# Attention plus MLP on one core: the position-bias hidden layer is made per distance instead of per key column

## The chip, the cores and the metric

The program runs on one core of a Trainium2 chip. The metric is the device time of one launch in microseconds (us); the kernel before takes 705.3 us (median of three runs, 705.29 to 706.06). A core has TensorE (PE, the matrix engine; PEld are its weight loads), VectorE (DVE), ScalarE (ACT), GpSimd (POOL), and SyncE (SP), which here only issues transfers. Sixteen DMA engines move the data.

## The reference

Attention over 4 batches, 8 heads, 576 positions and 64 channels, with a learned position bias, and then a two-layer block on the result. What matters here is the bias:

```python
rel = (pos[:, None] - pos[None, :]).astype(np.float32)
psi_rel = np.log1p(np.abs(rel))
psi_i = np.log1p(np.maximum(pos[:, None].astype(np.float32), 1.0))
x = (psi_rel / psi_i)[..., None]
h = np.maximum(x @ w1 + b1, 0.0)      # 32 hidden units
bias = h @ w2                         # 8 heads
scores = scores + bias.transpose(2, 0, 1)[None, :, :, :]
```

So `bias[i, j]` depends on the row `i` and on the distance `|i - j|` alone. The softmax, the product with v and the block `h * clip(h + 3, 0, 6) / 6 @ w_out` follow.

## The kernel before, in words

The bias is the same for all batches. It is made once, written to a table in DRAM (`bias_d`, five tiles of up to 128 rows), and loaded from there tile by tile when the softmax needs it.

It is made in 36 groups of 16 rows. Dividing by `psi_i` is left to the end: the kernel takes `relu(w1 * log1p(distance) + b1 * psi_i)` and scales by `1 / psi_i` when it evicts. `T` holds `w1 * log1p(|column - 572 - a|)`, 1148 columns wide, 32 hidden units by four rows (`a`) on 128 partitions, so a slice of 576 columns that starts at `572 - i0` is the row `i0 + a` over all keys. Each group has four steps:

- `z_group` (L827): four instructions of 128 x 576, each of four rows, dealt to DVE (L837) and ACT (L841); for groups 0 to 15 they take turns, later DVE takes two of three. 85 are on DVE and 59 on ACT.
- `bias_mm` (L845, L854): TensorE multiplies by `w2`. Each of the four results `z` goes to 32 of the 128 output partitions, in two halves of 288 columns, in f32: eight products, which the chip runs as 16 weight loads and 16 matmul instructions.
- `bias_out` (L860, L870): ACT evicts with scale and bias into `bo`; one instruction of 576 columns, or two of 288 once the kernel is in its steady stage (11 groups).
- `bias_store` (L873, L876): one transfer of 288 KB from `bo` to the table, issued on ACT's queue.

Groups 0 to 15 are made in the first 53 us, beside the preparation of `w_in` (L245 to L269, L122, L139) and the first tiles of attention. The other 20 run between 166 and 300 us, between the products of the block (L772, L795). `load_bias` (L466, L486, L483) loads the table on SP's queue.

The program is written as steps on one list, and a planner orders each engine's instructions by priority and by a simulated timeline. From tile 45 on TensorE and SP keep the order of the list (`keep_order`, L1083). How often a bias step is taken is set by the rates in `CFG`. Before any of this, `T` is loaded in two transfers (L1009, L1016) and scaled by `w1` in two DVE instructions (L1024).

Of the kernel before, what the change touches and what calls it, by code (L numbers as in the profile page):

```python
# [10 lines left out]
F32 = mybir.dt.float32  # L11
# [4 lines left out]
ALU = mybir.AluOpType  # L16
AX = mybir.AxisListType

S = 576
D = 64  # L20
H = 8
PAIRS = H // 2
HALF = S // 2
LT = 1148
NG = S // 16
CQ = 2.0 ** -25
VC = 5 * 128
# [6 lines left out]
def attention_moe_kernel(  # L34
# [15 lines left out]
    nc = tc.nc  # L50
# [15 lines left out]
    hl_p = ctx.enter_context(tc.tile_pool(name="hl", bufs=5))  # L66
    sm_p = ctx.enter_context(tc.tile_pool(name="sm", bufs=6))
    dr_p = ctx.enter_context(tc.tile_pool(name="dr", bufs=1, space=bass.MemoryType.DRAM))
# [11 lines left out]
    def s_bank(name):  # L80
        return pools["ps_s"].tile([128, 2, 512], F32, tag="s", name=name)
# [6 lines left out]
    def w_bank(name):  # L88

        if name == "o_ps":  # L90
            out_open[:] = [True, 0]
        elif out_open[0] and steady[0]:
            while out_open[0] and out_open[1] == 3:
                next(queue[0])
            out_open[1] += 1
        return pools["ps_w"].tile([128, 512], F32, tag="w", name=name)
# [3 lines left out]
    r_sb = const.tile([128, 2, 2 * PAIRS * 4], F32, name="r_sb")  # L100
    wi = big.tile([128, 2, KC, DFF], F16, name="wi")
    wo = big.tile([128, 2, KF, DM], F16, name="wo")
    bias_d = [dr_p.tile([H, min(128, S - i), S], F32, name=f"bias{i}") for i in range(0, S, 128)]

    ones_sb = const.tile([1, 128], F32, name="ones_sb")
    b1_sb = const.tile([128, 1], F32, name="b1_sb")
    w2_sb = const.tile([128, 32], F32, name="w2_sb")
# [3 lines left out]
    def halves(t):  # L111
        return t.rearrange("p (a b) -> p a b", a=2)
# [110 lines left out]
    def dq(c):  # L223
        return nc.scalar if c in cfg["act"] else nc.sync
# [241 lines left out]
    def load_bias(b, p, i):  # L466
        out = b_p.tile([128, 2 * S], F32, tag="bt", name="bt")
        src = [out[:, s * S:(s + 1) * S] for s in range(2)]
        if (p, i) in KEEP:
            if b:  # L470
                return out, kept[p, i]
            tag = KEEP[p, i]
            if tag == "z":
                t = z_e[:, p // 2]
            else:
                t = (const if tag[0] == "k" else pools["e"]).tile(
                    [128, 2 * S], F32, tag=tag, name=f"k{p}{i}"
                )
            src = [t[:, s * S:(s + 1) * S] for s in range(2)]
            kept[p, i] = src  # L480
        table = bias_d[i][2 * p:2 * p + 2]
        if i == 4:
            d = dq("b").dma_start(out=out[:, 0:S], in_=table.rearrange("h i j -> (h i) j"))  # L483
        else:
            whole = t if (p, i) in KEEP else out
            d = dq("b").dma_start(  # L486
                out=whole.rearrange("i (h j) -> i h j", h=2), in_=table.rearrange("h i j -> i h j")
            )
        bias_loads.append(d.ins)
        return out, src  # L490
# [321 lines left out]
    def zeng(g, k):  # L812
        pat = cfg["zeng"] if g >= cfg["gz2"] else cfg["z1"] if g >= cfg["gz"] else cfg["z0"]
        return pat[(4 * g + k) % len(pat)]

    def pattern(g):
        return tuple(zeng(g, k) != "A" for k in range(4))
# [6 lines left out]
    bias_t = {}  # L824
    emitted = [0, 0, 0, 0]

    def z_group(g):  # L827
        zs = []
        for k in range(4):
            i0 = 16 * g + 4 * k  # L830
            col = slice(i0 // 4, i0 // 4 + 1)
            src = T[:, 572 - i0:572 - i0 + S]
            if k % 2 == 0:
                z2 = (z_a if phase == 0 and g % 2 else z_e)[:, k // 2]
            z = z2[:, (k % 2) * S:(k % 2 + 1) * S]
            if zeng(g, k) == "D":
                nc.vector.tensor_scalar(  # L837
                    out=z, in0=src, scalar1=nbp[:, col], scalar2=None, op0=ALU.max
                )
            else:  # L840
                nc.scalar.activation(out=z, in_=src, func=AF.Relu, bias=bp[:, col])  # L841
            zs.append(z)
        bias_z[g] = zs

    def bias_mm(g):  # L845
        if steady[0]:
            pss = [w_bank("b_ps") for _ in range(2)]
        else:
            ps = s_bank("b_ps")
            pss = [ps[:, 0], ps[:, 1]]  # L850
        zs = bias_z.pop(g)
        for a in range(2):
            for k, z in enumerate(zs):
                nc.tensor.matmul(  # L854
                    out=pss[a][32 * k:32 * k + 32, 0:HALF], lhsT=w2_sb,
                    rhs=z[:, a * HALF:(a + 1) * HALF],
                )
        bias_ps[g] = pss if steady[0] else ps

    def bias_out(g):  # L860
        ps = bias_ps.pop(g)
        t = hl_p.tile([128, S], F32, tag="hl", name="bo")
        c = pats.index(pattern(g))
        cv, sc = cv_sb[:, c:c + 1], isc[:, g:g + 1]
        if isinstance(ps, list):
            ev = [(t[:, a * HALF:(a + 1) * HALF], ps[a][:, 0:HALF]) for a in range(2)]
        else:
            ev = [(halves(t), ps[:, :, 0:HALF])]
        for dst, src in ev:
            nc.scalar.activation(out=dst, in_=src, func=AF.Identity, scale=sc, bias=cv)  # L870
        bias_t[g] = t

    def bias_store():  # L873
        g = emitted[3]
        r0 = (16 * g) % 128
        dq("o").dma_start(  # L876
            out=bias_d[g // 8][:, r0:r0 + 16].rearrange("h i j -> i h j"), in_=bias_t.pop(g)
        )
        emitted[3] += 1

    def bias_step():
# [13 lines left out]
    def bias_next():  # L895
        z, m, o, d = emitted
        z_group(z)
        bias_mm(m)
        emitted[0] += 1
        emitted[1] += 1  # L900
        if o < m:
            bias_out(o)
            emitted[2] += 1
            bias_store()
# [16 lines left out]
    def front(n):  # L921
# [25 lines left out]
        while len(bt_t) - freed[0] < 4 and len(bt_t) < len(keys):  # L947
            k, b, p, i = keys[len(bt_t)]
            if k - n > (cfg["la"] if n > 3 else 2):
                break  # L950
            bias_until(128 * i + 128 if i < 2 else S)
            bt_t[b, p, i] = load_bias(b, p, i)
# [48 lines left out]
    T = pools["e"].tile([128, 2 * S], F32, tag="T", name="T")  # L1001
# [4 lines left out]
    isc = pools["e"].tile([128, NG], F32, name="isc")  # L1006
    w1_sb = pools["e"].tile([128, 1], F32, name="w1_sb")
    c36 = const.tile([128, 2], F32, name="c36")
    nc.sync.dma_start(out=T[:, 512:LT], in_=ltab[:, 512:LT])  # L1009
    nc.sync.dma_start(out=w1_sb, in_=w1c)  # L1010
    nc.sync.dma_start(out=b1_sb, in_=b1c)
    nc.sync.dma_start(out=bp, in_=psi)
    nc.sync.dma_start(out=w2_sb, in_=w2b)
    nc.sync.dma_start(out=isc, in_=ipsi)
    nc.sync.dma_start(out=eye_sb, in_=eye)
    nc.sync.dma_start(out=T[:, 0:512], in_=ltab[:, 0:512])  # L1016
    nc.vector.memset(cv_sb, 0.0)
    nc.vector.memset(ones_sb, 1.0)
    nc.vector.memset(c36[:, 0:1], 3.0 * CQ)
    nc.vector.memset(c36[:, 1:2], 6.0 * CQ)  # L1020
    for r in range(2):
        nc.gpsimd.memset(tq[r].bitcast(F32), 0.0)
    for cs in (slice(512, LT), slice(0, 512)):
        nc.vector.tensor_scalar(  # L1024
            out=T[:, cs], in0=T[:, cs], scalar1=w1_sb, scalar2=None, op0=ALU.mult
        )
    nc.vector.tensor_scalar(out=bp, in0=bp, scalar1=b1_sb, scalar2=None, op0=ALU.mult)
    nc.vector.tensor_scalar(out=nbp, in0=bp, scalar1=-1.0, scalar2=None, op0=ALU.mult)
    nc.vector.tensor_scalar(out=w2_sb, in0=w2_sb, scalar1=8.0, scalar2=None, op0=ALU.mult)
# [9 lines left out]
    for c, pat in enumerate(pats):  # L1039
        for k in range(4):  # L1040
            if pat[k]:
                rows = slice(32 * k, 32 * k + 32)
# [102 lines left out]
    for n in range(-1, NT + 7):  # L1145
# [17 lines left out]
        if done is not None and done != (0, 0):  # L1163
            b, u = done
# [20 lines left out]
def _layout(q, k, v, w1, b1, w2, moe_w_in, moe_w_out):  # L1185
    import numpy as _np

    Bn = q.shape[0]
    qt, kt = (x.transpose(0, 1, 3, 2).reshape(Bn, PAIRS, 128, S) for x in (q, k))
    qk = _np.concatenate([qt[..., :256], kt, qt[..., 256:]], axis=3)  # L1190
    rows = _np.arange(128)[:, None] + 128 * _np.arange(5)[None, :]
    rows[64:, 4] -= 64
    vr = v[:, :, rows.reshape(-1), :].reshape(Bn, PAIRS, 2, 128, 5, D)
    vp = vr.transpose(0, 1, 3, 4, 2, 5).reshape(Bn, PAIRS, 128, VC)
    w1c = _np.tile(w1.reshape(32, 1), (4, 1))
    b1c = _np.tile(b1.reshape(32, 1), (4, 1))
    w2b = _np.zeros((128, 32), dtype=w2.dtype)
    for a in range(4):
        w2b[32 * a:32 * a + 32, 8 * a:8 * a + 8] = w2
    a = _np.repeat(_np.arange(4), 32)  # L1200
    col = _np.arange(LT)
    ltab = _np.log1p(_np.abs(col[None, :] - 572 - a[:, None]).astype(_np.float32))
    pos = _np.arange(S).astype(_np.float32)
    psi = _np.log1p(_np.maximum(pos, _np.float32(1.0)))
    inv = (1.0 / psi.astype(_np.float64)).astype(_np.float32)
    row = _np.arange(128)
    ipsi = inv[16 * _np.arange(NG)[None, :] + (row // 32 * 4 + row % 32 // 8)[:, None]]
    psi = psi[4 * _np.arange(S // 4)[None, :] + a[:, None]]
    d = {
        "qk": qk, "vp": vp, "w1c": w1c, "b1c": b1c, "w2b": w2b,  # L1210
        "ltab": ltab.astype(_np.float32), "psi": psi, "ipsi": ipsi,
        "eye": _np.eye(128, dtype=_np.float32),
        "w_in": moe_w_in.view(_np.int64), "w_out": moe_w_out.view(_np.int64),
    }
    return {n: _np.ascontiguousarray(d[n]) for n in _INS}
# [20 lines left out]
```

## Time and profile before

| | us |
|---|---|
| median of three runs | 705.3 |
| the profiled execution | 701.48 |
| its span, first to last instruction | 699.5 |
| TensorE busy | 647.4 (93%) |
| VectorE busy | 487.8 (70%) |
| ScalarE busy | 488.6 (70%) |
| GpSimd busy | 252.7 (36%) |
| mean granted TensorE clock | 0.98 of full speed |

The share of busy time is a mean over stages. Until some 80 us TensorE is not the busiest engine, and after 300 us it hardly stops. A table by stretches says more than the shares.

### The profile page before, as it was taken

To read this page: it belongs to the slowest core of one execution; us is meant where nothing else is said; L and a number is where in the kernel's file an instruction comes from. 1 tells how busy PE (TensorE), PEld (TensorE's weight loads), DVE (VectorE), ACT (ScalarE), POOL (GpSimd) and SP (SyncE) were. 2 spreads that over 40 slices of the span, in tenths; PEclk is the share of its full clock that TensorE was granted. 3 is DMA by queue.
4 is the path that set the end of the run, shared out by engine and by line. 5 is a ranking of instruction groups with operands and counts; after the bars stand their busy time and mean duration, and the time that the engine had idled before them with its cause. 6 is when DMAs were issued, how large, how long until landed. Compare 5 with 4: busy or idle time off the path is not lost. (4 is left out here: it accounts for less than half of the span.)

```text
span 699.5 us, 15122 instructions
## 1 busy us (share of the span) xinstructions
PE 647.4 (93%) x5538; PEld 469.3 (67%) x5538; DVE 487.8 (70%) x1159; ACT 488.6 (70%) x963; POOL 252.7 (36%) x334
## 2 busy tenths in 40 slices
PE   7566899988899999999898899999999999999998
PEld 2234566765486667688787788767776777777775
DVE  7889869998776797667777877777677767410310
ACT  7986777978756998677768776886678856621620
POOL 2113121756302443145444552565236512410420
PEclk9988999999999999999999999999999999999999
DMA  8899867750999959898999699879896776100000
GB/s 266 280 356 344 277 227 272 262 193 4 229 241 228 256 117 261 230 236 184 236 276 247 143 207 220 200 146 199 171 202 132 162 149 130 21 10 29 1 10 28
DMA packets 177017, 129.08 MB, mean 185 GB/s; under 512 B 137776, under 2 KB 146224, under 8 KB 175920
## 3 DMA queue, kind: packets, MB, share of 16 engines
q1 hardware_dynamic: 167152, 112.79, 64.4%
q10 hardware_dynamic: 9792, 15.34, 7.2%
q8 instruction: 43, 0.70, 0.4%
q14 instruction: 30, 0.25, 0.1%
HBM read 76.19 MB, written 15.34 MB: 131 GB/s over the span
## 5 line engine op out<-in xcount | busy, mean ns | idle before, releaser
L772 PE MATMUL h_ps<-x,wi 128*128 128x256 f16 (+1 forms) x1536 | 202.6, 290 | 8.6 <-DVE t L755 3.9
L795 PE MATMUL o_ps<-g,wo 128*128 128x256 f16 (+1 forms) x1536 | 195.5, 286 | 0.8 <-DVE g L120 0.4
L772 PEld LDWEIGHTS <-wi 128*128 128x128 f16 x1536 | 149.2, 99 | 56.2 <-issue 13.9
L795 PEld LDWEIGHTS <-wo 128*128 128x128 f16 x1536 | 147.3, 98 | 46.0 <-issue 8.3
L751 POOL TENSOR_TENSOR g<-t,g 128x256 f16<-128x256 f32 (+1 forms) x128 | 102.5, 810 | 135.9 <-ACT g L749 134.9
L565 ACT ACTIVATE bt<-bt,sm 128x576 f32<-128x576 f32 x144 | 110.7, 769 | 52.5 <-DVE sm L554 49.7
L139 DVE SCALAR_TENSOR_TENSOR hl<-bt,sm,hl 128x576 f16<-128x576 f32 x112 | 99.6, 903 | 25.6 <-ACT hl L122 13.1
L755 DVE SCALAR_TENSOR_TENSOR t<-t,t,h_ps 128x320 f32<-128x320 f32 (+1 forms) x112 | 56.2, 515 | 63.8 <-ACT t L762 61.8
L116 POOL TENSOR_SCALAR hl<-bt,sm 128x576 f16<-128x576 f32 x56 | 45.0, 805 | 105.6 <-DVE sm L577 59.6
L749 ACT ACTIVATE g<-t 128x256 f16<-128x256 f32 (+1 forms) x128 | 55.8, 440 | 35.9 <-DVE t L755 35.4
L554 DVE CUSTOM_DVE_ANT_0 bt<-s_ps,bt 128x576 f32<-128x576 f32 x88 | 64.8, 749 | 10.0 <-PE s_ps L542 5.2
L762 ACT ACTIVATE t<-h_ps,t,hr 128x320 f32<-128x320 f32 (+1 forms) x112 | 64.8, 586 | 8.4 <-PE h_ps L772 6.0
L411 POOL TENSOR_TENSOR qkl<-st,qkh 128x576 fp32r<-128x576 f32 (+2 forms) x48 | 55.9, 1187 | 26.1 <-ACT qkh L404 25.5
L805 ACT ACTIVATE ot<-o_ps,os 128x256 f32<-128x256 f32 (+1 forms) x32 | 15.9, 497 | 58.1 <-PE o_ps L795 54.8
L854 PE MATMUL b_ps<-z_e,w_sb 128*32 128x288 f32 x448 | 44.1, 430 | 9.9 <-ACT bo L870 4.2
L573 DVE TENSOR_SCALAR sm<-sm 128x1 f32<-128x1 f32 x112 | 16.7, 150 | 43.6 <-ACT bt L565 43.6
L520 PE MATMUL s_ps<-qk 128*128 128x288 f32 x128 | 40.2, 439 | 7.3 <-ACT atf L616 2.6
L122 ACT ACTIVATE hl<-bt,sm 128x576 f16<-128x576 f32 x56 | 43.0, 770 | 5.5 <-issue 1.2
L837 DVE TENSOR_SCALAR z_e<-T,nbp 128x576 f32<-128x576 f32 x69 | 37.8, 595 | 5.4 <-PE b_ps L854 5.4
L841 ACT ACTIVATE z_e<-T,bp 128x576 f32<-128x576 f32 x43 | 32.0, 767 | 7.9 <-PE b_ps L854 4.1
L542 PE MATMUL s_ps<-qkh 64*128 64x288 f32 x192 | 30.4, 346 | 6.6 <-DVE sm L554 6.3
L870 ACT ACTIVATE bo<-b_ps,cv_sb,isc 128x576 f32<-128x576 f32 (+1 forms) x47 | 33.2, 709 | 4.2 <-DMA at<-hl 2.2
(128 smaller groups left out, 881.9 us busy)
## 6 DMA issues: line engine op xcount, KB each, us to landing
bt<-bias SPq DMA_DIRECT2D x36, 576.0 KB, 5.3
bias<-bo ACTq DMA_DIRECT2D x36, 288.0 KB, 5.4
w<-in_w_in_dram SPq DMA_DIRECT2D x8, 1024.0 KB, 6.6
vs<-in_vp_dram SPq DMA_DIRECT2D x24, 320.0 KB, 4.9
st<-in_qk_dram SPq DMA_DIRECT2D x16, 448.0 KB, 4.3
wo<-in_w_out_dram SPq DMA_DIRECT2D x5, 1024.0 KB, 7.1
bt<-bias SPq DMA_DIRECT2D x16, 288.0 KB, 3.7
va<-in_vp_dram SPq DMA_DIRECT2D x12, 320.0 KB, 6.3
```

The lines of the kernel that those rows point to most:

```text
L116: nc.gpsimd.tensor_scalar(out=out, in0=full, scalar1=scale, scalar2=1.0, op0=ALU.mult, op1=ALU.mult)
L139: nc.vector.scalar_tensor_tensor(out=out, in0=full, scalar=scale, in1=high, op0=ALU.mult, op1=ALU.subtract)
L411: nc.gpsimd.tensor_sub(out=lo[:, c:c + w], in0=t[:, c:c + w], in1=hi[:, c:c + w].bitcast(F32))
L554: nc.vector.tensor_tensor_reduce(out=halves(bt), in0=ps, in1=halves(src), op0=ALU.add, op1=ALU.min, scale=-0.125, scalar=3.0e38, accum_out ...
L565: nc.scalar.activation(out=bt, in_=bt, func=AF.Exp, scale=-1.0, bias=sm[:, 0:1], accum_out=total)
L749: nc.scalar.activation(out=g[:, 0], in_=uu, func=AF.Copy)
L751: e.tensor_sub(out=g[:, 1], in0=uu, in1=g[:, 0])
L755: nc.vector.scalar_tensor_tensor(out=t_t[f], in0=t_t[f], scalar=cols(f)[2], in1=h_t.pop(f)[:, 0:n], op0=ALU.min, op1=ALU.mult,)
L762: nc.scalar.activation(out=t_t[f], in_=h_t[f][:, 0:n], func=AF.Relu, scale=cols(f)[0], bias=cols(f)[1],)
L772: nc.tensor.matmul(out=h_t[f][:, 0:n], lhsT=wi[:, a, c, f * 128:(f + 1) * 128], rhs=x[:, e, c], start=(k == 0), stop=(k == 3 * KC - 1),)
L795: nc.tensor.matmul(out=ops[:, 0:n], lhsT=wo[:, a, f, e * 128:(e + 1) * 128], rhs=g_t[f][:, r], start=(f == 0 and a == 0 and r == 0), stop= ...
L854: nc.tensor.matmul(out=pss[a][32 * k:32 * k + 32, 0:HALF], lhsT=w2_sb, rhs=z[:, a * HALF:(a + 1) * HALF],)
```

## The change

The hidden layer is now taken over distances 0 to `w - 1`, where `w` is one more than the largest distance in the group: `576 - 16g` for groups 0 to 17, `16g + 16` from 18 on. `T` shrinks to 576 columns, the same in all four rows of a partition group. The product reads `z` backwards for the keys on the left of the diagonal and forwards for those on the right, 591 columns in all, and cuts them where the direction turns and where a PSUM bank ends: two pieces for groups 4 to 31, three for the other eight. Row `r` of a group then stands shifted by `r`; the store undoes that by stepping one element more per row in a DRAM table whose rows are 608 wide.

```diff
-LT = 1148
+BW = S + 15
+BP = 608
...
-    bias_d = [dr_p.tile([H, min(128, S - i), S], F32, name=f"bias{i}") for i in range(0, S, 128)]
+    bias_d = [dr_p.tile([H, min(128, S - i), BP], F32, name=f"bias{i}") for i in range(0, S, 128)]
...
-        table = bias_d[i][2 * p:2 * p + 2]
+        table = bias_d[i][2 * p:2 * p + 2, :, 16:16 + S]
...
-            src = T[:, 572 - i0:572 - i0 + S]
+            w = max(16 * g + 15, S - 1 - 16 * g) + 1
+            src = T[:, 0:w]
...
-            z = z2[:, (k % 2) * S:(k % 2 + 1) * S]
+            z = z2[:, (k % 2) * S:(k % 2) * S + w]
...
+    def bias_cut(g):
+        left = 16 * g + 15
+        return left, min(max(left, BW - 512), 512)
...
-        for a in range(2):
+        left, first = bias_cut(g)
+        cuts = sorted({0, left, first, BW})
+        for lo, hi in zip(cuts, cuts[1:]):
+            c = 512 - first + lo if lo < first else lo - first
             for k, z in enumerate(zs):
                 nc.tensor.matmul(
-                    out=pss[a][32 * k:32 * k + 32, 0:HALF], lhsT=w2_sb,
-                    rhs=z[:, a * HALF:(a + 1) * HALF],
+                    out=pss[int(lo >= first)][32 * k:32 * k + 32, c:c + hi - lo], lhsT=w2_sb,
+                    rhs=z[:, left - lo:left - hi:-1] if lo < left else z[:, lo - left:hi - left],
                 )
...
-        t = hl_p.tile([128, S], F32, tag="hl", name="bo")
+        t = hl_p.tile([128, BW], F32, tag="hl", name="bo")
...
+        first = bias_cut(g)[1]
         if isinstance(ps, list):
-            ev = [(t[:, a * HALF:(a + 1) * HALF], ps[a][:, 0:HALF]) for a in range(2)]
+            ev = [(t[:, 0:first], ps[0][:, 512 - first:]), (t[:, first:], ps[1][:, 0:BW - first])]
         else:
-            ev = [(halves(t), ps[:, :, 0:HALF])]
+            ev = [(t, ps.rearrange("p a b -> p (a b)")[:, 512 - first:512 - first + BW])]
...
-        dq("o").dma_start(
-            out=bias_d[g // 8][:, r0:r0 + 16].rearrange("h i j -> i h j"), in_=bias_t.pop(g)
-        )
+        rows = bias_d[g // 8][:, r0:r0 + 16, 1:1 + BW].rearrange("h i j -> i h j")
+        step, *rest = rows.ap
+        dst = bass.AP(rows.tensor, rows.offset, [[step[0] + 1, step[1]], *rest])
+        dq("o").dma_start(out=dst, in_=bias_t.pop(g))
...
-    nc.sync.dma_start(out=T[:, 512:LT], in_=ltab[:, 512:LT])
+    nc.sync.dma_start(out=T[:, 0:S], in_=ltab)
...
-    nc.sync.dma_start(out=T[:, 0:512], in_=ltab[:, 0:512])
...
-    for cs in (slice(512, LT), slice(0, 512)):
-        nc.vector.tensor_scalar(
-            out=T[:, cs], in0=T[:, cs], scalar1=w1_sb, scalar2=None, op0=ALU.mult
-        )
+    nc.vector.tensor_scalar(out=T[:, 0:S], in0=T[:, 0:S], scalar1=w1_sb, scalar2=None, op0=ALU.mult)
```

## Rows read from the trace of the kernel before

**Rows 1.** The page's first part: busy time, share, instructions of each engine.

```profile
PE 647.4 (93%) x5538; PEld 469.3 (67%) x5538; DVE 487.8 (70%) x1159; ACT 488.6 (70%) x963; POOL 252.7 (36%) x334
```

**Rows 2.** Busy time by stretch (us from the start); the first line names the columns.

```profile
core 0: us, PE busy (x) PEld busy (x) DVE busy (x) ACT busy (x) POOL busy (x), PEclk, DMA share, GB/s
0.00:30.00 30.00, 21.16 (x172) 8.19 (x176) 24.50 (x58) 24.79 (x33) 7.05 (x17) 1.00 0.87 296
30.00:40.00 10.00, 3.68 (x44) 1.33 (x36) 7.25 (x11) 8.12 (x13) 1.20 (x1) 0.74 0.74 250
40.00:80.00 40.00, 30.50 (x176) 19.05 (x169) 39.72 (x88) 31.65 (x52) 8.36 (x10) 0.89 0.91 328
80.00:100.00 20.00, 20.00 (x138) 12.26 (x136) 13.81 (x39) 14.32 (x26) 4.27 (x6) 1.00 0.74 251
100.00:160.00 60.00, 54.89 (x389) 41.17 (x388) 56.26 (x122) 50.10 (x95) 28.04 (x24) 0.97 0.66 229
160.00:180.00 20.00, 17.03 (x140) 11.42 (x139) 18.18 (x41) 15.03 (x30) 9.83 (x11) 0.91 0.19 39
180.00:300.00 120.00, 112.78 (x1133) 81.00 (x1133) 87.31 (x216) 91.69 (x177) 38.22 (x48) 0.99 0.95 226
300.00:700.00 400.00, 387.34 (x3367) 294.87 (x3365) 240.79 (x588) 252.94 (x543) 155.72 (x219) 1.00 0.66 145
```

**Rows 3.** Waits of DVE from 4 to 52 us: total, times, longest.

```profile
DVE bt L554 <- DMA bt<-bias: 2.7, 1, 2.7
...
DVE vparts L178 <- DMA vf<-in_vp_dram: 1.4, 1, 1.4
```

**Rows 4.** Groups of instructions, shapes kept apart: count | busy, mean ns | idle before.

```profile
L837 DVE TENSOR_SCALAR z_e<-T,nbp 128x576 f32<-128x576 f32 x69 | 37.8, 595 | 5.4 <-PE b_ps L854 5.4
L841 ACT ACTIVATE z_e<-T,bp 128x576 f32<-128x576 f32 x43 | 32.0, 767 | 7.9 <-PE b_ps L854 4.1 <-DVE bp L1027 2.9 <-DVE w2p L162 0.8
L870 ACT ACTIVATE bo<-b_ps,cv_sb,isc 128x576 f32<-128x576 f32 x25 | 20.4, 821 | 3.3 <-DMA at<-hl 2.2 <-PE b_ps L854 1.0
...
L870 ACT ACTIVATE bo<-b_ps,cv_sb,isc 128x288 f32<-128x288 f32 x22 | 12.8, 582 | 0.9 <-ACT ot L805 0.5 <-DMA bias<-bo 0.2 <-PE b_ps L854 0.2
...
L1024 DVE TENSOR_SCALAR T<-T,w_sb 128x636 f32<-128x636 f32 x1 | 0.6, 550 | 2.3 <-DMA w_sb<-in_w1c_dram 2.3
L1024 DVE TENSOR_SCALAR T<-T,w_sb 128x512 f32<-128x512 f32 x1 | 0.5, 478 | 0.0
```

**Rows 5.** Timeline at the start, SP and DVE: start us, us, instruction.

```profile
4.01 0.43 SPq L1016 DMA_DIRECT2D T<-in_ltab_dram  x1
...
6.93 0.48 DVE L1024 TENSOR_SCALAR T<-T,w_sb 128x512 f32<-128x512 f32 x1
```

**Rows 6.** Bias products from 160 to 300 us: durations ns min/median/max, first and last start.

```profile
L854 PEld LDWEIGHTS b_ps<-z_e,w_sb x320: 106/109/178, 169.0 to 296.9; 128*32 128x32 f32 x160
L854 PE MATMUL b_ps<-z_e,w_sb x320: 406/406/689, 169.0 to 297.2; 128*32 128x288 f32 x160
```

**Rows 7.** Timeline: one group's products (start us, us; 16 instructions merged).

```profile
250.35 1.18 PE L854 MATMUL b_ps<-z_e,w_sb 128*32 128x288 f32 x16
```

**Rows 8.** Waits of PE from 160 to 300 us: total, times, longest.

```profile
PE b_ps L854 <- DVE z_e L837: 2.1, 2, 1.1
PE b_ps L854 <- ACT bo L870: 1.8, 1, 1.8
PE b_ps L854 <- ACT z_e L841: 0.8, 1, 0.8
```

**Rows 9.** The page's transfers: issuer, count, KB each, median us to landing.

```profile
bt<-bias SPq DMA_DIRECT2D x36, 576.0 KB, 5.3
bias<-bo ACTq DMA_DIRECT2D x36, 288.0 KB, 5.4
...
T<-in_ltab_dram SPq DMA_DIRECT2D x1, 318.0 KB, 2.9
T<-in_ltab_dram SPq DMA_DIRECT2D x1, 256.0 KB, 2.8
```

More of the change, by code (lines that the diff above doesn't have):

```diff
@@ L1200, in _layout @@
     a = _np.repeat(_np.arange(4), 32)
-    col = _np.arange(LT)
-    ltab = _np.log1p(_np.abs(col[None, :] - 572 - a[:, None]).astype(_np.float32))
+    ltab = _np.broadcast_to(_np.log1p(_np.arange(S).astype(_np.float32)), (128, S))
     pos = _np.arange(S).astype(_np.float32)
```

## The prediction

> **What bounds the kernel now.** I read the shares first: TensorE is busy 93% of the span, DVE and ACT 70% each [rows 1]. Such a mean hides stages, so next I read busy time by stretch [rows 2]. Three regimes show. Up to 80 us TensorE is not the bound: it is busy 21.2 of the first 30 us and 3.7 of the next ten, while the DMA share is 0.87 at 296 GB/s, and from 40 to 80 us DVE works 39.7 of 40 us. From 100 to 180 us DVE is still the fullest beside TensorE (18.2 of 20 us from 160 on). From 180 us TensorE leads (112.8 of 120 us) and after 300 us it is busy 387 of 400. The bias work lies in the first regime (groups 0 to 15, up to 53 us) and from 166 to 300 us (groups 16 to 35). So what the change takes from DVE and ACT counts early, and what it adds to TensorE counts late. Then the waits: before 52 us DVE idles 2.7 us for the first bias load and 1.4 us for v [rows 3]; from 160 to 300 us TensorE waits 2.9 us, in three pieces, for `z` from DVE or ACT and 1.8 us for an eviction [rows 8].
>
> **The change part by part.**
>
> *The table T.* One load and one DVE instruction go: the second part, 0.48 us [rows 5], and 60 columns of the first. Two widths of this instruction give DVE's price per column: (550 - 478) / 124 = 0.58 ns [rows 4], so 0.03 us more; 0.51 us in all. The transfers shrink from 318 + 256 KB to 288 KB [rows 9], about 1.0 us at the 296 GB/s of that stretch [rows 2], and SP issues its first `w_in` load 0.43 us earlier [rows 5]. The first scaling does not move: it waits for `w1` [rows 4], not for T.
>
> *The hidden layer.* Instruction count stays at 144; each shrinks from 576 to `w` columns. Saved columns: 896 on DVE and as many on ACT in groups 0 to 7 (16 instructions each), 2944 each in groups 8 to 15, then 7936 on DVE (53 instructions) and 3968 on ACT (27). ACT's price per column from its evictions is (821 - 582) / 288 = 0.83 ns [rows 4]. DVE therefore saves 0.52 + 1.71 + 4.60 us and ACT 0.74 + 2.44 + 3.29 us. The bounds of a column on DVE are 0 and 595 / 576 = 1.03 ns [rows 4], as the trace has no narrower `z`; I take 0.58, the same operation between the same memories.
>
> *What of it counts early.* The wait of 2.7 us for the first bias load [rows 3] hangs on group 7's store, so up to it only what that store gains counts: T and groups 0 to 7, about 1.0 us on DVE and 0.6 on ACT, less the longer products of groups 0 to 3 (below). I take 0.7 us. After that wait DVE is full until 80 us, and there the eight `z` of groups 12 to 15 (1728 columns) give 1.0 us. Sum 1.7 us, bounds 0 (transfers keep the pace: 328 GB/s from 40 to 80 us [rows 2]) and 0.51 + 0.52 + 1.71 = 2.7. When DVE's stretch ends earlier, TensorE, full from 80 to 100 us [rows 2], is late next, and passes the gain on.
>
> *What of it counts later.* Groups 16 to 19 lose 2896 columns on DVE, 1.7 us, in the stretch where DVE has 18.2 of 20 us; about half is on the path, 0.8 us. Behind each of TensorE's three waits for `z` [rows 8] stand about two instructions, so each wait shrinks by some 0.15 us: 0.4. Sum 1.2 us; bounds 0, and 1.7 + 2.9 = 4.6. The rest lies under TensorE's work.
>
> *The products.* A group runs as passes of four matmuls side by side. Its 16 instructions last 1.18 us [rows 7] and one matmul 0.406 [rows 6], so the four passes start (1.18 - 0.406) / 3 = 0.258 us apart: 0.9 ns per column. A group now streams 591 columns twice: +15 x 2 x 0.9 = 0.03 us. [...] Groups 16 to 35 then add 0.3 + 0.25 + 1.3 = 1.9 us, where TensorE has no cover. Bounds: 0.5 us (20 groups x 0.03, columns alone) and some 9 us, if each of the 24 short passes there took a whole 0.406.
>
> The row shows 109 ns for a weight load whatever follows it [rows 6]. [...] No row here shows a short pass.
>
> *Reading backwards.* No row has a moving operand with a negative step. Bounds: nothing, or twice the forward rate on the reversed columns, 8460 in groups 16 to 35: 8460 x 2 x 0.9 ns = 15.2 us. I take nothing, the forward rate being the only row [rows 7]; the other end is a rival.
>
> *Eviction, store, load.* Fifteen columns more are 12 ns per eviction on ACT, 0.2 us up to 53 us and under TensorE's work later. 36 stores and all loads stay in number and on their queues (ACT's and SP's); a store carries 2364 instead of 2304 bytes per row, +2.6%. The stores hold no wait that was not there: the eviction before them ends where its last product ends. I cost them at nothing as long as the landing stays near 5.4 us [rows 9].
>
> *Sum.* -1.7 - 1.2 + 1.9 = -1.0 us against the profiled 701.48, that is 700.5. The median of the runs is 3.8 us above that execution, so the forecast is 704.3. Its own range: from -2.7 - 4.6 + 0.5 to 0 + 0 + 2.2 (passes with a little more than a weight load each), 698.5 to 707.5.
>
> **The rivals.**
>
> *A. The early gain is larger.* The planner orders DVE, ACT and POOL anew with the shorter instructions and fills the holes of the first 80 us (DVE idles 5.5 us in the first 30, 2.75 from 30 to 40 [rows 2]). For: all engines wait on each other there. Against: DMA at 296 GB/s is close to the 328 of the later stretch. All of 2.7, half of the wait for the first load (1.4) and 2 of the later 4.6, less 1.9 for TensorE: -4.2 us, 701.1.
>
> *B. Reading backwards is slow.* Place: left pieces of groups 16 to 35 in TensorE's own stretch, where it idles only 7 of 120 us [rows 2]. At twice the time: 15.2 us, less the 1.0 forecast and some 2 us of idle time: +12 us, 717. It decides from a slowdown of (1.0 + 1.4) / 15.2 = 16% of the reversed columns; below that the result is no change. For: nothing measured. Against: the forward pass leaves no sign of a memory limit.
>
> *C. The gains stay covered.* The early stretch keeps the pace of its transfers, the planner's new order costs as much as it gives, and TensorE pays its 1.9 us: +2 us, 707.3.
>
> *D. Rows off the grid.* A stored row now starts at any multiple of 4 bytes, and rows are loaded 2432 bytes apart. If loads and stores took a tenth longer (5.3 and 5.4 us [rows 9]), the first load and some later ones would land 0.5 us later each: 0 net of the gains, 705.3; if a store had to wait for the one before, ACT would stand with it, up to 5 us in the first stretch: +4. The nearest row speaks against a price: T's rows were 4592 bytes apart and its 318 KB landed in 2.9 us [rows 9]. [...]
>
> *E. Short passes cost only their columns.* If weights for a short pass are in place before it is due, the products add the lower bound, 0.5 us: -1.7 - 1.2 + 0.5 = -2.4 us, 702.9. For: a weight load runs beside the matmuls of the pass before, and takes less than half of one [rows 6]. Against: a short pass leaves no time to hide the next load.
>
> *The change does nothing.* If `z` of 320 columns took as long as one of 576, only T's 0.5 us would be left against 1.9: this ends within C.
>
> **How the numbers follow.** Forecast 0.38, A 0.18, B 0.10, C 0.14, D 0.08, E 0.12. A measurement of this kernel can tell 0.2% (1.4 us) from no change. Faster by more than that (below 703.9): A, 0.11 of E and 0.12 of the forecast, whose range leans to that side, 0.41. Within: 0.25 of the forecast, 0.01 of E, 0.04 of C, 0.02 of D, 0.32. Slower: B, 0.10 of C, 0.06 of D, 0.01 of the forecast, 0.27. The range goes from 699, below A, to 710; it leaves out B, the ends of A and D, and the far end of the short passes, 0.17 together.
>
> **What would show it.** `z` of group 17 (304 columns) at about 0.36 us on DVE and 0.54 on ACT; T scaled once. Passes of 512 forward and of left pieces at 0.9 ns per column alike; short passes 0.11 us apart, groups 32 to 35 near 1.5 us to the end of the last product. The first softmax of the table some 0.7 us before 37.5 us, and TensorE's full stretch beginning 1.7 us before 80. Busy TensorE after 300 us unchanged. Wrong if reversed passes are longer than forward ones, if stores land well after 5.4 us, or if TensorE's idle time changes where no bias work is: then the order, not the work, made the difference.

## The result and the profile after

The change is slower. In five runs it took 713.15 us at the median against 705.3, a ratio of 1.0102 (95% interval 1.0058 to 1.0146), and in the first experiment 1.0110 (1.0072 to 1.0148). The profiled execution of after took 706.67 us, 6.5 below its median; so the two profiles differ by 5.2 us where the medians differ by 7.9, and ratios of many runs carry the verdicts below. One per cent is 7.0 us.

The work went down about as forecast. The page's first part of the kernel after, to be set against [rows 1]: DVE has 9.5 us less (the savings of the prediction add up to 7.3), ACT 5.8 less (6.5), TensorE 2.7 more.

```profile
PE 650.1 (92%) x5602; PEld 472.3 (67%) x5602; DVE 478.3 (68%) x1158; ACT 482.8 (69%) x963; POOL 245.2 (35%) x334
```

Busy time by stretch of the kernel after, columns as in [rows 2]; the last three lines are cut more finely than there:

```profile
0.00:30.00 30.00, 19.81 (x190) 7.17 (x192) 23.34 (x57) 23.50 (x32) 7.17 (x17) 0.90 0.86 284
30.00:40.00 10.00, 8.31 (x62) 3.60 (x56) 8.89 (x20) 9.10 (x15) 1.37 (x1) 0.80 0.79 249
40.00:80.00 40.00, 28.37 (x155) 17.63 (x156) 37.61 (x78) 29.80 (x50) 6.57 (x10) 0.79 0.92 333
160.00:180.00 20.00, 18.28 (x163) 11.74 (x165) 15.21 (x41) 13.36 (x30) 6.15 (x10) 1.00 0.20 42
180.00:300.00 120.00, 109.35 (x1087) 80.13 (x1084) 79.35 (x203) 85.47 (x168) 36.56 (x46) 0.94 0.90 217
300.00:700.00 400.00, 390.31 (x3416) 297.97 (x3417) 243.03 (x595) 255.92 (x549) 157.84 (x220) 1.00 0.68 147
...
180.00:187.60 7.60, 5.70 (x49) 2.92 (x45) 3.54 (x13) 5.39 (x12) 1.35 (x2) 1.00 1.20 271
187.60:201.20 13.60, 10.53 (x51) 7.09 (x51) 11.11 (x35) 10.26 (x18) 6.12 (x6) 0.50 0.86 220
201.20:300.00 98.80, 93.12 (x990) 70.13 (x990) 64.70 (x157) 69.82 (x140) 29.09 (x38) 1.00 0.89 212
```

TensorE's busy time from 180 to 300 us fell from 112.8 to 109.4 although it has more to do there, and within that, from 187.6 to 201.2 us, its clock was granted at 0.50 of full speed, after it had stood idle for 1.67 us up to 187.39. Where is it held up? The timeline of the kernel after, by engine (DVE, ACT, POOL, PE):

```profile
187.25 0.15 DVE L160 COPY p_w<-m_ps 128x1 f32<-128x1 f32 x1
...
190.50 1.95 DVE L141 SCALAR_TENSOR_TENSOR hl<-bt,sm,hl 128x576 f16<-128x576 f32 x1 [2.49 <-POOL hl L118]
192.37 0.15 DVE L219 RECIPROCAL rm_w<-p_w 128x1 f32<-128x1 f32 x1
...
195.00 0.22 DVE L221 TENSOR_SCALAR r_w2c<-w2p,rm_w 128x8 f32<-128x8 f32 x1
...
182.11 0.84 ACT L882 ACTIVATE bo<-b_ps,cv_sb,isc 128x591 f32<-128x591 f32 x1 [3.51 <-DMA at<-hl]
...
195.87 0.71 ACT L124 ACTIVATE g<-g,r_w2c 128x512 f16<-128x512 f16 x1
...
189.72 0.75 POOL L118 TENSOR_SCALAR hl<-bt,sm 128x576 f16<-128x576 f32 x1 [4.18 <-DMA bias<-bo]
...
187.39 0.71 PE L544 MATMUL s_ps<-qkh 64*128 64x288 f32 x2 [1.67 <-DVE sm L556]
...
190.85 2.20 PE L865 MATMUL b_ps<-z_e,w_sb 128*32 128x335 f32 x16 [1.79 <-ACT bo L882]
194.33 0.84 PE L544 MATMUL s_ps<-qkh 64*128 64x288 f32 x2 [1.28 <-DVE sm L556]
...
197.75 4.47 PE L797 MATMUL o_ps<-g,wo 128*128 128x256 f16 x24
```

The same place in the kernel before (ACT, DVE, POOL, PE):

```profile
180.99 0.83 ACT L870 ACTIVATE bo<-b_ps,cv_sb,isc 128x576 f32<-128x576 f32 x1 [2.21 <-DMA at<-hl]
...
187.93 0.16 DVE L158 COPY p_w<-m_ps 128x1 f32<-128x1 f32 x1 [1.62 <-PE m_ps L155]
...
188.55 0.23 DVE L219 TENSOR_SCALAR r_w2c<-w2p,rm_w 128x8 f32<-128x8 f32 x1
...
188.57 0.77 POOL L116 TENSOR_SCALAR hl<-bt,sm 128x576 f16<-128x576 f32 x1 [2.62 <-PE m_ps L155]
...
191.50 0.50 PE L795 MATMUL o_ps<-g,wo 128*128 128x256 f16 x3
```

`r_w2c` scales `g`, and `g` opens the second layer's products `o_ps`. From `p_w`, which it comes from, to `r_w2c` DVE took 0.62 us before and takes 7.75 now, though `p_w` is ready 0.7 us earlier. In between stand two `z`, a split tile `hl` that waits for POOL, a reduction, a softmax and a split of v, none of them a new instruction: the planner put them there. TensorE's own order has moved too: one more group of bias products and more scores (`s_ps`) now stand ahead of `o_ps`, and they wait 1.67, 1.79 and 1.28 us for a softmax, an eviction and a softmax. When `o_ps` starts at 197.75 us it waits for nothing, as its first `g` has stood since 196.6. So this trace does not say how much of the delay is the late `g` and how much TensorE's own queue; both are the planner's order. DVE's wait of 2.49 us for POOL comes through a shared buffer. The evicted bias tile `bo` and the split tiles (`hl`, `xr`) take turns in five buffers (tag `hl`); the eviction of group 17 waits 3.51 us until a transpose has read one of them, and POOL's next `hl` waits 4.18 us until that group's store has left it.

### The profile page after: what moved, and what is told of

The parts are those of the page before. It is cut to its first block, busy times and chain, and to the rows that moved or that the text cites. A ratio compares the mean times of both kernels' runs of the same rounds, so it can differ in the third digit from the quotient of the medians.

```text
span 704.7 us, 15238 instructions
## 1 busy us (share of the span) xinstructions
PE 650.1 (92%) x5602; PEld 472.3 (67%) x5602; DVE 478.3 (68%) x1158; ACT 482.8 (69%) x963; POOL 245.2 (35%) x334
## 5 line engine op out<-in xcount | busy, mean ns | idle before, releaser
L774 PE MATMUL h_ps<-x,wi 128*128 128x256 f16 (+1 forms) x1536 | 197.9, 286 | 7.1 <-DVE t L757 3.7
L774 PEld LDWEIGHTS <-wi 128*128 128x128 f16 x1536 | 146.9, 98 | 52.1 <-issue 11.7
L753 POOL TENSOR_TENSOR g<-t,g 128x256 f16<-128x256 f32 (+1 forms) x128 | 98.7, 781 | 130.6 <-ACT g L751 126.0
L865 PE MATMUL b_ps<-z_e,w_sb 128*32 128x512 f32 (+46 forms) x496 | 44.6, 441 | 13.2 <-ACT z_e L844 8.3
L882 ACT ACTIVATE bo<-b_ps,cv_sb,isc 128x591 f32<-128x591 f32 (+16 forms) x47 | 33.8, 720 | 9.6 <-PE b_ps L865 5.2
L865 PEld LDWEIGHTS b_ps<-z_e,w_sb 128*32 128x32 f32 x496 | 14.3, 117 | 35.4 <-ACT z_e L844 15.6
L840 DVE TENSOR_SCALAR z_e<-T,nbp 128x320 f32<-128x320 f32 (+17 forms) x69 | 32.8, 521 | 7.5 <-PE b_ps L865 7.5
```

Source lines behind the costliest of these rows:

```text
L753: e.tensor_sub(out=g[:, 1], in0=uu, in1=g[:, 0])
L774: nc.tensor.matmul(out=h_t[f][:, 0:n], lhsT=wi[:, a, c, f * 128:(f + 1) * 128], rhs=x[:, e, c], start=(k == 0), stop=(k == 3 * KC - 1),)
L865: nc.tensor.matmul(out=pss[int(lo >= first)][32 * k:32 * k + 32, c:c + hi - lo], lhsT=w2_sb, rhs=z[:, left - lo:left - hi:-1] if lo < left ...
```

## The experiments

All compare with runs of the kernel before on the same chip. Runs that are set beside each other often stand on different chips, so their ratios to before are compared, not their times. Intervals are 95%, and for a difference of two ratios I take the root of the sum of the squared half-widths. Theory T1: the planner's new order costs, not the work. Rival R1: the work costs (products, stores). Rival R2: the order costs, but in the first 100 us.

**Order and work exchanged.** At the end of the program each engine's instructions are chained in a given order, the one that the planner made for the other kernel:

```diff
+    impose_order(nc, tc)
...
+        for a, b in zip(picks, picks[1:]):
+            tc.add_manual_dep(
+                line[b], line[a].name,
+                mybir.DependencyInfo(mybir.DependencyClass.NoSync, mybir.DependencyReason.DATA),
+                reason="issue order",
+            )
```

The control lays before's own order on before.

> Control: the kernel before, with its own order laid on every engine in the way that the runs with an exchanged order had theirs. Every theory: 1.000 of before, within its interval. If it is off by 0.4% or more, laying an order on the engines costs time by itself, and the runs with an exchanged order must be read against this one.

Measured 0.9999 (0.9977 to 1.0020): laying an order on costs nothing that +-0.2% can show. Its profile also says how far one execution can be trusted: the same program in the same order has a span of 701.9 us instead of 699.5, and from 30 to 40 us its granted clock is 0.89 instead of 0.74. The others:

> The changed kernel as it is, a second time, so that the three others have it beside them on the same chip. Theory T1 (the planner's new order of instructions around 180 to 200 us, not the work, costs the time) and rival R1 (the work itself costs: reversed and three-piece products, stores and loads off the grid): both 1.010 of before again, 707 to 715 us. Its trace shows the first product into o_ps some 6 us later than in before (191.5) and a stretch at the lower granted clock between 185 and 205 us by T1.

> All the work of the change (T, narrower z, passes of two or three pieces, shifted stores and loads), but on every engine the instructions are issued in the order that they have in the kernel before; where the change has more products, they stand where their group's products stood. T1: no slower than before, 1 to 4 us faster (701 to 704 us beside 705), because the work went down by 10 us on DVE and 6 on ACT and up by 3 on TensorE; the first product into o_ps within 1 us of 191.5. R1: as slow as the changed kernel, 1.008 to 1.012 of before.

> All the work of the kernel before (576-column z, passes of 288), but on every engine in the order that the planner gave to the changed kernel. T1: slower than before by 5 to 12 us (710 to 717), with the same late o_ps and idle TensorE around 185 to 200 us. R1: 705, as before.

> The work of the change; the order of the changed kernel up to the first h_ps product (some 103 us), the order of the kernel before from there on. T1 (loss lies at 180 to 200 us): as fast as the change in the old order throughout, 700 to 704 us, perhaps 1 us faster as the weights are made earlier. Rival R2 (the loss lies in the first 100 us, where the first softmax comes 4.8 us later and the lower clock lasts longer): slower than the old order throughout by 4 us or more.

Measured: after again 1.0110; the change's work in the old order 1.0062 (1.0034 to 1.0089), 709.5 us; the old work in the new order 1.0149 (1.0116 to 1.0181), 715.0 us; new order up to 103 us, then the old one, 1.0056 (1.0026 to 1.0085). T1 is half right: the new order costs the old work 1.5% and the changed work 0.5% (+-0.5). R2 falls: the new first part costs nothing that shows (1.0056 beside 1.0062, +-0.4% on the difference). But the work in the old order is not the gain that T1 asked for; it is a loss of 0.6%, so T1 alone does not do. R1 alone does not either, as it asked for the whole 1%. About half of the loss comes with the order and half with the work.

**A buffer of its own for one bias tile.** Theory T2: the loss at 180 to 200 us comes through the shared buffers. By it their waits go and the products `o_ps` behind them come earlier: 704 to 706 us in the old order (709.5 with the shared buffer); in the new order `o_ps` some 3 us earlier and 706 to 709 us.

```diff
+        if g == 17:
+            t = const.tile([128, 2 * S], F32, tag="kb1", name="bo")[:, 0:BW]
+        else:
+            t = hl_p.tile([128, BW], F32, tag="hl", name="bo")
```

> As work_oldorder (work of the change, order of before), but the evicted bias tile of group 17 goes to a buffer of its own, one that nothing else uses before 260 us, in place of one of the five buffers that it shares with the split attention tiles. [...] Rival R1 (the products and stores themselves cost): 709, unchanged. Rival R3 (several small losses before 180 us, 2.4 us in that trace, with the lower clock): 707 to 708.

> The changed kernel in its own order, with the same one buffer for the bias tile of group 17. [...] T1 alone (the new order as such, whatever the buffers): no change, 712 to 713.

> The work and order of the kernel before, with the buffer of its own for group 17's bias tile. In the trace of before this store had landed at 188.4 us, 0.2 us ahead of the split tile that reuses its buffer, so T2 expects little: 703 to 705 us, 0.998 to 1.002. If it gains 2 us or more, the buffer is worth as much without the change, and the change is to be set against this kernel.

> The changed kernel with group 17's own buffer, in its own order up to the first h_ps product (some 103 us) and in the order of before from there. The order costs 4 us more with that buffer (707.9 against 703.9). If they are lost after 103 us (T1 with T2): 702 to 704.5 us. If before (R2): 707 to 708.5.

> The changed kernel with group 17's own buffer, where the planner makes its order anew with that buffer in view; nothing laid on the engines. If its order is free of the waits on shared buffers: 702 to 706 us. If the planner again puts the scaling of g late behind other work (T1): 707 to 712.

Measured: old order 1.0009 (0.9986 to 1.0032), new order 1.0063 (1.0035 to 1.0091), before itself 0.9955 (0.9927 to 0.9983), new order to 103 us 1.0014 (0.9984 to 1.0044), planned anew 1.0050 (1.0025 to 1.0076). The timeline of the old order with the change's work, first with the shared buffer (work_oldorder; ACT, POOL, PE):

```profile
183.32 0.84 ACT L1092 ACTIVATE bo<-b_ps,cv_sb,isc 128x591 f32<-128x591 f32 x1 [1.78 <-DMA at<-hl]
...
192.13 0.74 POOL L328 TENSOR_SCALAR hl<-bt,sm 128x576 f16<-128x576 f32 x1 [4.92 <-DMA bias<-bo]
...
191.61 0.49 PE L1007 MATMUL o_ps<-g,wo 128*128 128x256 f16 x3 [0.77 <-ACT g L334]
195.97 4.43 PE L1007 MATMUL o_ps<-g,wo 128*128 128x256 f16 x20 [3.87 <-DVE g L332]
```

and with the tile's own (oldorder_own_bo):

```profile
180.21 0.84 ACT L1095 ACTIVATE bo<-b_ps,cv_sb,isc 128x591 f32<-128x591 f32 x1
...
184.59 0.74 POOL L328 TENSOR_SCALAR hl<-bt,sm 128x576 f16<-128x576 f32 x1
...
192.26 7.94 PE L1007 MATMUL o_ps<-g,wo 128*128 128x256 f16 x56 [2.65 <-ACT g L334]
```

With the shared buffer `o_ps` begins at 191.61 us, as T1 had it, and then stands 3.87 us for the next `g`; with the tile's own it begins at 192.26 and runs on. The waits for `at<-hl` and `bias<-bo` are gone, as T2 said, and the three pairs with the change's work gain 0.42 to 0.53% (+-0.4 to 0.5 on each), some 3.3 us. But before gains as much (0.45%, +-0.28), where I expected nothing: there too the eviction stood 2.2 us for the buffer. So sharing is a cost of either kernel, not the change's own; T2 does not explain the difference between them. In the new order the gain came although `o_ps` starts no earlier (200.13 us, below), against what T2 had expected. New order to 103 us was expected in times that fit neither outcome; by its ratio it stands beside the old order (1.0014 and 1.0009), so the loss lies behind 103 us. Planned anew, the order is again late (`o_ps` at 200.6 us).

**Which stretch of the order.**

> The changed kernel with group 17's own buffer, in its own order up to the 150th h_ps product (some 166 us), in the order of before from there. With the switch at 103 us it was 1.0014, with its own order throughout 1.0063. T1 (the order between 166 and 230 us, where g is scaled late, costs): 0.999 to 1.003. Rival: the order between 103 and 166 us costs: 1.005 to 1.008.

Measured 0.9959 (0.9935 to 0.9982), 701.9 us: faster than both kernels, and than T1 expected. Beside the switch at 103 us (1.0014) the new order from 103 to 166 us is a gain of 0.55% (+-0.38). Against the new order throughout (1.0063, same buffer) the order after 166 us is worth 1.04% (+-0.37), 7.3 us. The timeline of DVE and PE with the new order throughout (neworder_own_bo):

```profile
190.27 0.76 DVE L772 CUSTOM_DVE_ANT_0 bt<-s_ps,bt 128x576 f32<-128x576 f32 x1 [1.99 <-DMA bt<-bias]
...
190.95 0.15 DVE L376 COPY p_w<-m_ps 128x1 f32<-128x1 f32 x1
...
195.07 0.64 DVE L437 TENSOR_SCALAR r_w2c<-w2p,rm_w 128x8 f32<-128x8 f32 x1
...
195.60 2.20 PE L1081 MATMUL b_ps<-z_e,w_sb 128*32 128x335 f32 x16 [3.13 <-ACT bo L1101]
...
200.13 1.25 PE L1013 MATMUL o_ps<-g,wo 128*128 128x256 f16 x5
```

and with the old order from 166 us (neworder_to_166):

```profile
186.20 0.16 DVE L376 COPY p_w<-m_ps 128x1 f32<-128x1 f32 x1 [1.32 <-PE m_ps L373]
...
186.83 0.22 DVE L437 TENSOR_SCALAR r_w2c<-w2p,rm_w 128x8 f32<-128x8 f32 x1
...
192.49 8.71 PE L1013 MATMUL o_ps<-g,wo 128*128 128x256 f16 x63 [2.53 <-ACT g L340]
```

With the old order `r_w2c` comes 0.63 us behind `p_w` again, `p_w` itself no longer stands behind a softmax that waits 1.99 us for a load of the table, no wait of 3.13 us of bias products stands ahead of `o_ps`, and `o_ps` starts 7.6 us earlier. The two orders differ until some 230 us and hardly after (6 places on DVE, 14 on ACT), so the loss lies between 166 and 230 us, where T1 put it. The switch changes all five engines' orders at once: which of these waits is worth how much is not shown.

Is the work a gain in an order that suits it? The old work in this order with this buffer:

> The work of the kernel before in the order and with the buffer of neworder_to_166 (0.9959 of before with the change's work). If the change's work is a gain in an order made for it, as the forecast's early and later gains say (2.9 us less 0.5 for products): 0.998 to 1.003. If the work is worth nothing in any order: 0.993 to 0.997.

Measured 1.0025 (1.0005 to 1.0045). With the same buffer the change's work is thus 0.66% (+-0.31) faster than the old work in this order, and 0.54% (+-0.36) slower in the order of before. The difference between the two is 1.20% (+-0.47): what the work is worth depends on the order, and the two cannot be priced one by one. It is not that each order suits the durations that it was made with: the planner's whole order for the changed work is 0.54% (+-0.36) slower for that work than the old one.

**The products.** In the old order, each piece read forwards, or fewer pieces:

```diff
-        cuts = sorted({0, left, first, BW})
+        cuts = [0, first, BW]
...
-                    rhs=z[:, left - lo:left - hi:-1] if lo < left else z[:, lo - left:hi - left],
+                    rhs=z[:, 0:hi - lo],
```

This is oldorder_forward, and with the tile's own buffer oldorder_own_bo_forward. forward_three keeps the first line, reversed_two has `z[:, first:0:-1] if lo < first` in the last, ahead of the forward reading. All four leave out part of the bias.

> As work_oldorder, but each group's products are two forward passes from column 0 of z, 591 columns in all: no reversed reading and no third, short pass. It leaves out the mirrored half of the bias, so its output is not the reference's; instructions, evictions, stores and loads stay as many. T1 and T2: 0 to 1 us under work_oldorder, 708.5 to 709.5. R1: the loss goes, 703 to 705.

> As oldorder_own_bo (703.9 us), but each group's products are two forward passes from column 0 of z; it leaves out the mirrored half of the bias. In the traces the products of groups 16 to 35 take 28.0 us with reversed and short passes and 27.5 with two forward ones: if only that counts, 703 to 704 us. R1, the size that oldorder_forward showed against work_oldorder (3 us): 700 to 701.5 us.

> As oldorder_own_bo (1.0009 of before), with the change's own cuts (two or three pieces, 40 groups of short passes in all places where the change has them) but every piece read forwards from column 0 of z; it leaves out the mirrored half of the bias. Two forward pieces measured 0.9934. If reading backwards costs (rival B of the forecast): 0.992 to 0.996. If the third, short passes cost: 0.999 to 1.002. If both, between.

> As oldorder_own_bo_forward (0.9934 of before), two pieces per group, but the first one is read backwards (from its last column down), the second forwards; it leaves out part of the bias. If reading backwards costs: 0.998 to 1.002. If the third, short passes cost: 0.992 to 0.996.

Measured 1.0019 (0.9993 to 1.0046); then, all with the own buffer, two forward pieces 0.9934 (0.9908 to 0.9961), three forward 0.9986 (0.9959 to 1.0012), two with the first reversed 0.9947 (0.9919 to 0.9975), beside 1.0009 of the full products. Over these four, which stand on three chips, reading backwards costs 0.18% (+-0.26), not told from nothing, and the third pieces 0.57% (+-0.26), 4 us. One more reading is on a single chip: with two forward pieces the change's work stands at 0.9934 and the old work, in the same order and with the same buffer, at 0.9955. So without reversed and third pieces the work is 0.21% (+-0.39) faster, 1.5 us; the forecast gains less the longer columns, -1.7 - 1.2 + 0.5 us, lie within this, and shifted stores and loads, which that run keeps, cost at most little. In the old order it is the third pieces that turn the work into a loss. Their busy time does not show it. A three-piece group of forward_three and a two-piece one of oldorder_own_bo_forward, timelines of PE:

```profile
295.51 1.21 PE L1075 MATMUL b_ps<-z_e,w_sb 128*32 128x512 f32 x24
```

```profile
295.76 1.20 PE L1074 MATMUL b_ps<-z_e,w_sb 128*32 128x512 f32 x16
```

Where are the 4 us? The third pieces lie in groups 0 to 3 and 32 to 35:

```diff
+        two = g < 4
+        cuts = [0, first, BW] if two else sorted({0, left, first, BW})
...
+                    rhs=z[:, 0:hi - lo] if two and hi - lo == 79 else z[:, left - lo:left - hi:-1] if lo < left else z[:, lo - left:hi - left],
```

> As oldorder_own_bo (1.0009 of before), but groups 0 to 3 make their product in two pieces (the first reads z forwards from column 0, so the mirrored part of their bias is left out); groups 32 to 35 keep three. The third pieces of all eight groups cost 0.57% together in the factorial of four runs. If they cost in the first 30 us, where each group's store is waited for: 0.995 to 0.997. If they cost at 255 to 290 us, where TensorE is full: 0.999 to 1.002.

> The other half: groups 32 to 35 in two pieces (the last 79 columns read from column 0 of z; part of their bias is left out), groups 0 to 3 in three. If the third pieces cost early: 0.999 to 1.002; if late: 0.995 to 0.997. If both near 0.998, they share it.

Measured 1.0004 (0.9976 to 1.0033) and 0.9992 (0.9956 to 1.0027), the latter with `g >= 32`. Inconclusive: each lies where its expectation blames the third pieces that were left in. Taking away one half gives back 0.05% or 0.17%, with +-0.4 on each, which neither adds up to 0.57% nor excludes it. Whether third pieces cost as much in the planner's own order was not run.

## Why the prediction failed

- **The step that failed: the sum had no term for the planner's order.** It priced edits as if each instruction stayed in its place, and left the order to rival C, "the planner's new order costs as much as it gives", at +2 us and a chance of 0.14. In the kernel as it is the new order cost 0.48% (+-0.47), 3.4 of the 7.7 us that 1.10% are. In the kernel with the tile's own buffer it cost 7.3 us after 166 us and gave back 0.55%, 3.9 us, between 103 and 166. The last sentence of the prediction named the order, without a price, and looked for it in idle time where no bias work is; the loss stands between 166 and 230 us, where bias work runs.
- **The other half failed with every instruction in its place.** That is the case that the sum priced: -1.0 us, and the old order with the change's work cost +0.62% (+-0.28), 4.4 us. The term that was too small there is the third pieces: 1.3 us for groups 32 to 35, and for groups 0 to 3 a deduction within the early 0.7, against 4 us (+-1.8) measured for all eight groups. How they cost it stays open.
- **Early gain, -1.7: not seen.** In the new order DVE is idle more, not less, from 40 to 80 us (37.6 busy, 39.7 before), and the clock there is 0.79 instead of 0.89. In the old order the place can be compared. Wait for the first bias load and busy time from 40 to 80 us, of work_oldorder:

```profile
DVE bt L766 <- DMA bt<-bias: 4.9, 1, 4.9
...
40.00:80.00 40.00, 30.07 (x181) 18.35 (x174) 38.03 (x80) 30.85 (x54) 7.68 (x10) 0.90 0.95 337
```

and of own_order, the program of before once more:

```profile
DVE bt L769 <- DMA bt<-bias: 3.2, 1, 3.2
...
40.00:80.00 40.00, 29.40 (x177) 17.93 (x177) 39.10 (x82) 31.84 (x53) 8.01 (x10) 0.90 0.96 348
```

  DVE has its 1 us less to do, and waits 1.7 us longer for the load, with the transfers at 337 and 348 GB/s: this fits the lower bound, 0, "transfers keep the pace". One profile of each cannot tell a gain below a microsecond or two.
- **Later gain, -1.2: in the new order the waits moved.** TensorE's waits from 160 to 300 us in the kernel after, to [rows 8]:

```profile
PE s_ps L544 <- DVE sm L556: 3.8, 3, 1.7
...
PE b_ps L865 <- ACT bo L882: 1.8, 1, 1.8
PE s_ps L544 <- ACT bo L882: 1.8, 1, 1.8
...
PE b_ps L865 <- ACT z_e L844: 0.6, 1, 0.6
```

  Those for `z` fell from 2.9 to 0.6 us, more than forecast; waits for a softmax (`sm`) and for an eviction of the bias stand in their place.
- **The hidden layer: right in size.** Over all its instructions DVE saves 6.9 us and ACT 6.8, where 6.8 and 6.5 were forecast. Three groups of instructions of the kernel after, as in [rows 4]:

```profile
L840 DVE TENSOR_SCALAR z_e<-T,nbp 128x304 f32<-128x304 f32 x5 | 2.1, 467 | 1.1 <-PE b_ps L865 1.1
...
L840 DVE TENSOR_SCALAR z_e<-T,nbp 128x352 f32<-128x352 f32 x5 | 1.7, 392 | 0.0
...
L844 ACT ACTIVATE z_e<-T,bp 128x304 f32<-128x304 f32 x3 | 1.5, 539 | 0.7 <-PE b_ps L865 0.7
```

  0.58 ns per column from 478 gives 0.385 us at 352 columns on DVE (0.392 measured); 0.54 us at 304 columns on ACT was forecast. On DVE 0.36 us was forecast at 304 columns; three of the five take that (0.359 to 0.364), but the mean is 0.467, as one took 0.869; what stretched it these rows do not name.
- **Products, +1.9: mis-sized in busy time.** The timeline of PE after, groups of two and three pieces, to [rows 7]:

```profile
276.39 1.21 PE L865 MATMUL b_ps<-z_e,w_sb 128*32 128x511 f32 x16
...
283.96 1.24 PE L865 MATMUL b_ps<-z_e,w_sb 128*32 128x512 f32 x24
```

  The third piece adds 0.03 us or less to a group, where the 1.3 us of the sum for four groups take 0.33 each. The terms 0.25 and 1.3 us count at least one weight load, 0.11 us, for each pass: no run shows such a floor. In the group of three pieces at 283.96 us the last four passes start from 284.85 to 284.97, 28 to 59 ns apart, and its weight loads last 106 to 113 ns; this is nearer rival E's price. The ends of matmuls are modelled, but the starts agree: the next instruction starts 1.13 us behind the first product of the group of two pieces, 1.18 behind that of three, and 1.14 in the next group of three that no wait cuts. Yet in time the third pieces cost 0.57% in the old order, which neither the sum nor E had; its cause is open.
- **Reading backwards, stores and loads at nothing: right** within the errors. Rival B's 15.2 us fall (0.18% +-0.26, 1.3 us), and D's slower landings; a landing after takes 5.3 and 5.5 us, to [rows 9]:

```profile
bt<-bias SPq DMA_DIRECT2D x36, 576.0 KB, 5.5
bias<-bo ACTq DMA_DIRECT2D x36, 295.5 KB, 5.3
```

  The first two loads of the table do land later, in 7.1 us instead of 5.7. That this is the order's doing is my reading. With the change's work in the old order (work_oldorder) the two loads from 174 to 200 us land in 5.7 us, where before has 6.5, and the stores there in 6.1 (two of them), where before has 5.2 (four): no price of the shifted rows shows in the loads, and for the stores these few leave it open. "The stores hold no wait that was not there" overlooked who waits for the store: the next tile in the shared buffers. [rows 4] had the sign, 2.2 us of idle time of the eviction put down to `at<-hl`; as shown above, the kernel before pays for this too.

## What to carry to other kernels

Where a planner orders the work, price its order as a term of its own: look which instruction opens the next full stretch of the bound engine, what stands between it and its source, and ask what other durations would put there. To part work from order, lay each kernel's order on the other and add a control; here that showed that the same work is a loss in one order and a gain in another. An idle time put down to a transfer of another tile can be the sign of a shared buffer; here one tile moved out of it was worth 0.45% without any change of the work.

The fastest kernels of the study that make the whole bias are the change with that buffer and the old order from 166 us (0.9959) and the kernel before with that buffer alone (0.9955). That the change is worth having beyond the buffer is not shown.

## What was not expected of the hardware

The time at the lower granted clock is no measure of the loss by itself. Over the runs of the first experiment the mean granted clock of after was 0.966 and of before 0.976, 49 and 34 us at the lower level (an estimate: twice one minus the clock, times the span, with 0.50 for the lower level, as from 187.6 to 201.2 us above, and 1.00 for the rest). But oldorder_own_bo_forward, at 0.9934 the fastest of all, has 0.970 and 43 us. So the time at that level does not put these kernels in their order; that it costs only where the rest waits for TensorE is my reading, and no run here prices it. Executions of the same program differ more than I had reckoned with: the 33 of before on one chip that enter the ratios went from 700.4 to 708.9 us.
